# Two layers of segmented attention and gated feed-forward on one core: a new opening, rows of two more norms turned by DMA, a new order of work

## Chip, cores, metric

The kernel runs on one core of a Trainium2 chip. A core has TensorE (PE; its weight loads are listed apart as PEld), VectorE (DVE), ScalarE (ACT), GpSimd (POOL) and SyncE (SP, whose queue issues nearly all transfers here), which run side by side and meet at semaphores. The metric is the device time of one execution in microseconds (us); lower is better.

## What is computed

An input x of 2048 rows and 512 columns (bfloat16) goes through attention, feed-forward, and both again with the same weights, each behind a layer norm without weights and each added to x:

```python
x = x + _A_ref(_layernorm(x, axis=-1), A_wq, A_wk, A_wv, A_wo, A_beta)
x = x + _B_ref(_layernorm(x, axis=-1), B_w_gate, B_w_up, B_w_down)
x = x + _A_ref(_layernorm(x, axis=-1), A_wq, A_wk, A_wv, A_wo, A_beta)
x = x + _B_ref(_layernorm(x, axis=-1), B_w_gate, B_w_up, B_w_down)
```

The attention has 32 heads of 16 columns and takes the rows in 4 segments of 512. Inside a segment it is causal softmax attention; beside it each head reads a 16x16 memory, to which every segment adds phi(k)ᵀ v, where phi(t) is t+1 for positive t and exp(t) otherwise:

```python
for s in range(N):
    logits = jnp.einsum('bhqd,bhkd->bhqk', qs, ks) * scale + mask
    a_dot = jnp.einsum('bhqk,bhkd->bhqd', _softmax(logits, axis=-1), vs)
    a_mem = num / den            # phi(q) @ M,  phi(q) @ z + 1e-6
    outs.append(g * a_mem + (1.0 - g) * a_dot)
    M = M + jnp.einsum('bhld,bhle->bhde', pk, vs)
```

The feed-forward is `_gelu(x @ w_gate) * (x @ w_up) @ w_down` with 1792 hidden columns.

## The kernel before

**Stages.** Layer and segment together give eight stages, k = 0 to 7. `Att(k)` normalizes 512 rows, makes q, k and v, takes 20 score steps, turns exp of the scores into weighted sums of v ("flush"), and reads and updates the memory. `Ffn(k)` multiplies by wo, adds to x, normalizes again and runs gate, up and down. Stage k+4 needs the rows that stage k has finished; the stages of one layer need each other only through the memory.

**How a norm's rows get turned.** A `Norm` has the key ("xnTa", k) for attention and ("xnTf", k) for the feed-forward. Per tile of 128 rows VectorE takes the statistics (L522, L531), GpSimd makes the scales (L539, L545), and VectorE writes the normalized rows xn (L559). Products need them transposed, in xnT. `row()` has two ways for that (L573 to 578). If the key is in `BY_PE`, four products with the identity on TensorE (line 498, in the groups m<-ident,xn) go into the list of items, and VectorE or ScalarE copies the result out of PSUM (L489, L490). Otherwise `turn_later` posts a transposing DMA to SP's queue (L463, xnT<-xn). Stage 0's attention norm is turned by hand in the opening (L602, L605, L607).

**Products.** Nearly all dense products go through `product` (L493 to 498): four matmuls, each a quarter of the array's columns, of up to 512 columns of the other operand. Score matmuls (L941) use another tiling, in which the array is cut by rows. A score step fills two PSUM buffers, st0 and st1, and ScalarE takes exp of each (L972); GpSimd masks the diagonal blocks (L959). The planner may visit both buffers of a step together or one after the other with other products between; the latter is called a halved step here.

**What sets the order.** The program is planned while it is built. `Clocks` keeps a clock for TensorE and one for each other engine (512 columns 0.2158 us, a change of tiling 0.102), and the loop at the end (L1364 to 1400) always asks what is next on TensorE: a score visit if its inputs and buffers are planned to be ready, else a started item, else the first item in order of its due time whose `ready` holds, else half a score step, else a filler, a product of ones (L1395, the group m<-warm of line 498) that keeps TensorE busy. Work for the other engines is posted as jobs with slacks. Due times are `DUE` and `DUE_STEP` by kind plus a correction by stage and index from `BIAS`. What runs on the chip is the resulting fixed order on each engine, with semaphores where one needs another.

**The opening** is written out by hand (L1239 to 1296): loads of x rows 0 to 3, wk and wq in two parts of columns each, x of segment 1, wv, in that order on SP; 19 products of ones (`WARM`, L404); then statistics, scales and rows of stage 0, their turns on TensorE, and the first block of q and k for stage 0. Then the planner's clocks are set by hand (L1292 to 1296) and the loop begins. Statistics of segments 1 and 2 are posted at fixed times (L1306, L1307), and the later loads are posted at fixed times too (L42).

The v item's due time and condition before:

```python
return Item(k - QK_DUE + bias("v", k, j) + DUE["v"] + 0.01 * j if k else -0.61,
            lambda: ck.has(("xnTa", k)) and (k < SETS or ("flush", k - SETS, 3, 1) in ev),
            dense(ps, pairs), done, kind="v", ps=ps)
```

Of the kernel before, what the change touches and what calls it, by code (L numbers as in the profile page):

```python
# [11 lines left out]
ACT = mybir.ActivationFunctionType  # L12
# [6 lines left out]
P = 128  # L19
# [4 lines left out]
NK = 2 * NSEG  # L24
L = 512
# [4 lines left out]
TPS = L // P  # L30
# [2 lines left out]
EPS_LN = 1e-5  # L33
EPS_MEM = 1e-6
MANUAL = {ENG.PE, ENG.Activation, ENG.SP, ENG.DVE, ENG.Pool}
WARM = 19
STEPS = 20
BY_PE = {("xnTf", 0), ("xnTf", 1), ("xnTf", NK - 1)}
M_BANKS = 4
PT_STEPS = 5  # L40
SETS = 3
# [3 lines left out]
N3 = 0.0  # L45
GELU_TILES = 2
QK_DUE = 0.655
E_Q = -0.378
E_K = 1.118

FLUSH_WAIT = 5.905
PIECE_SLACK = 3.609
URGENT, SOON, NORMAL = -11.1, -0.333, 0.0
EXP_SLACK, E_SLACK, PHI_SLACK, GELU_SLACK = -1.031, 6.011, 3.476, 3.142
ACT_EVICT, FIRST_EVICT = 3.886, 2.071
XN_BUFS = 4
XN_KEPT = 0
XNA1_PE = 0
NORM_HALVES = 8
KBP = 0  # L60
XNP = 0
RAWS = [7, 7, 8, 6, 8, 6, 8]
FLUSH_FIRST = -0.616
SECOND_EVICT = 0.639
E_BUFS = 2
KB_SLACK = 4.318
HALF_STEPS = 1
LAST_FIRST = 8
MARGIN = 1.0
PHI_MARGIN = 1.7  # L70
KB_MARGIN = 1.5
MEM_SLACK = -2.669


DUE = {"wo": 0.557, "gate": 1.085, "up": 1.338, "down": 1.877, "upd": 0.195, "mem": 0.129, "v": 0.157}
DUE_STEP = {"gate": 0.0119, "up": 0.0256, "down": 0.0162}
BIAS = {
    **{("qk", *k): d for k, d in {
        (0,): 0.054, (1,): 0.349, (1, 4): -0.115, (2,): 0.05, (3,): 0.031, (4,): -0.046, (5,): -0.12, (6,):
        0.194, (7,): 0.037, (7, 5): -0.014  # L80
    }.items()},
    **{("mem", *k): d for k, d in {
        (0,): -0.022, (0, 0): -0.039, (1,): -0.188, (2,): 0.215, (3,): 0.144, (4,): -0.223, (5,): -0.032,
        (6,): -0.036, (7,): -0.117
    }.items()},
    **{("down", *k): d for k, d in {
        (0,): 0.506, (1,): -0.623, (2,): -0.186, (3,): -0.143, (4,): -0.443, (5,): -0.102, (6,): 0.877, (6,
        2): 0.03, (7,): -0.082
    }.items()},
    **{("upd", *k): d for k, d in {  # L90
        (0,): -0.189, (1,): 1.254, (2,): -0.142, (3,): 1.042, (4,): -0.026, (5,): 0.508, (6,): 0.081, (7,):
        0.007
    }.items()},
    **{("v", *k): d for k, d in {
        (0,): 0.246, (1,): 0.279, (2,): 0.177, (3,): -0.1, (4,): -0.388, (4, 0): -0.03, (5,): -0.816, (6,):
        -0.162, (7,): 0.199
    }.items()},
    **{("wo", *k): d for k, d in {
        (0,): -0.36, (0, 0): -0.225, (1,): 0.135, (2,): -1.075, (3,): -0.773, (4,): -0.197, (5,): -0.803,
        (5, 2): -0.205, (6,): -0.181, (7,): -0.25  # L100
    }.items()},
    **{("gate", *k): d for k, d in {
        (0,): 0.131, (1,): -0.134, (2,): 0.56, (2, 5): 0.034, (3,): 0.122, (4,): -0.775, (4, 8): 0.253,
        (5,): -0.02, (6,): 0.694, (7,): -0.205
    }.items()},
    **{("up", *k): d for k, d in {
        (0,): 0.267, (1,): 0.175, (2,): -0.027, (3,): -0.044, (4,): -0.002, (4, 4): -0.286, (5,): -0.133,
        (6,): -0.52, (7,): -0.092
    }.items()},
    **{("num", *k): d for k, d in {  # L110
        (2, 0): -0.064, (3, 0): -0.003, (3, 2): -0.014, (4, 2): 0.171, (5, 2): -0.092
    }.items()},
    **{("ek", *k): d for k, d in {
        (1, 1): 0.005, (2, 1): -0.028
    }.items()},
    **{("eq", *k): d for k, d in {
        (3, 2): -0.036
    }.items()},
}

# [203 lines left out]
def kernel(  # L324
# [14 lines left out]
    nc = tc.nc  # L339
# [9 lines left out]
    ck = Clocks()  # L349
    ev = ck.ev  # L350
# [52 lines left out]

    keep_warm(WARM, 0)  # L404

# [32 lines left out]
    for va in vaugs:  # L438
        nc.scalar.activation(out=by_head(va)[:, :, :, DH], in_=cden[:].unsqueeze(1).to_broadcast([P, TPS, H]),
                             func=ACT.Copy)  # L440
# [5 lines left out]
    def later_constants():  # L446
# [5 lines left out]

        ck.pool.post(14.0, MEM_SLACK, (1.9, lambda: nc.gpsimd.memset(kBs[2][:], 0.0), None))
        for b in range(4):
            ck.pool.post(20.0 + 3.0 * b, MEM_SLACK, (0.5, lambda b=b: scale(b), None))

# [9 lines left out]
    banks = [0.0] * M_BANKS  # L466
# [13 lines left out]
    def evict(ps, dst, src, told, slack=NORMAL):  # L480
# [6 lines left out]

        first = FIRST_EVICT if ("scores", 0) not in ev else SECOND_EVICT if ("scores", 1) not in ev else ACT_EVICT
        ck.dve.post(ck.made(), slack, (0.673, lambda: nc.vector.tensor_copy(out=dst(), in_=src()), end), taken=taken)  # L489
# [18 lines left out]
    class Norm:  # L508
# [54 lines left out]
        def row(self, j, i, ready):  # L563
# [9 lines left out]
            def told(t):  # L573
                if self.key in BY_PE or XNA1_PE and self.key == ("xnTa", 1):
                    insert(self.turn_item(j, xn, t, landed))
# [43 lines left out]
    class Att:  # L619
# [13 lines left out]
        def add_items(self):  # L633
            k, s = self.k, self.s
# [18 lines left out]
            def q_done(b, ps):  # L653
                def told(t):
                    ev["q", k, b] = t
                    self.q_there[b // 2].append(t)
                    if s > 0 and len(self.q_there[b // 2]) == 2:
                        e_jobs.append((k - E_Q + bias("eq", k, b) + 0.03 * b, max(self.q_there[b // 2]),
                                       lambda: k < 2 or ("memn", k - (1 if s > 1 else 2)) in ev,
# [4 lines left out]
            def odd_heads(t):  # L664
# [11 lines left out]
                for g in range(4):  # L676
                    r = slice(32 * g + 16, 32 * g + 32)
                    ck.sp.post(t, KB_SLACK, (0.55, lambda r=r: nc.sync.dma_start(
                        out=self.kB[r], in_=self.kf[r]), lambda t2: ck.at(t2 + 1.8, lambda: landed(t2 + 2.0))))

            def k_done(b, ps, at=None):
                def told(t):
# [8 lines left out]
                    if s < NSEG - 1:  # L691
                        before = ("mem", k - 1) if s else ("mem", k - 2) if k else ("xnTa", 1)
                        e_jobs.append((k + E_K + bias("ek", k, b) + 0.03 * b, t, lambda: before in ev,
                                       lambda r, sl: self.phi_k(b, r, sl), True))
# [9 lines left out]
            def v(j):  # L704
                ps = Psum()
                pairs = [(lambda kt=kt: self.norm.xnT[:, kt, j * P:(j + 1) * P], lambda kt=kt: w_att["v"][:, kt, :])
                         for kt in range(KT)]

                def done():
                    self.counted()  # L710
                    evict(ps, lambda: by_head(self.vaug)[:, j, :, 0:DH],
                          lambda: ps()[:].rearrange("p (h e) -> p h e", e=DH),
                          lambda t: ev.update({("v", k, j): t}))

                return Item(k - QK_DUE + bias("v", k, j) + DUE["v"] + 0.01 * j if k else -0.61,
                            lambda: ck.has(("xnTa", k)) and (k < SETS or ("flush", k - SETS, 3, 1) in ev),
                            dense(ps, pairs), done, kind="v", ps=ps)

            for b in range(KT) if k else range(EARLY, KT):
# [128 lines left out]
        def upd_item(self):  # L848
# [13 lines left out]
            def done():  # L862
# [23 lines left out]
                else:  # L886
# [5 lines left out]
                             (0.2, z, told)]  # L892
                ck.dve.chain(ck.made(), MEM_SLACK, *steps)

            items.append(Item(k + DUE["upd"] + bias("upd", k), ready, [(Clocks.MM[128], lambda c=c: m(c)) for c in range(n_mm)],
                              done, kind="upd", ps=psm))
# [192 lines left out]
    class Ffn:  # L1089


        def __init__(self, k):
# [6 lines left out]
            self.n_gate, self.n_gel, self.kept = [0] * self.parts, [0] * self.parts, [[] for _ in range(self.parts)]  # L1099
            raw = RAWS[k] if self.parts == 1 else 0  # L1100

# [137 lines left out]
    n0 = att[0].norm  # L1239
# [27 lines left out]
    a0 = att[0]  # L1267
    a0.made()
    n0.first_rows = [n0.normed(j, j) for j in range(2)]
    gate()  # L1270
    n0.first_rows += [n0.normed(2, 2)]
    n0.first_turn(0)
    n0.first_turn(1)
    keep_warm(2, 0)
    ps = bank_tile(1, [P, L])
    a0.first_k(ps, 0, P)
    n0.first_turn(2)
    nc.vector.tensor_copy(out=a0.kf[:, 0, 0:P], in_=ps[:, 0:P])
    n0.first_rows += [n0.normed(3, 3)]
    n0.first_turn(3)  # L1280
    ps, half = bank_tile(2, [P, L]), L // 2
    a0.first_q(ps, 0, half)
    nc.scalar.activation(out=a0.q[:, 0, 0:half], in_=ps[:, 0:half], func=ACT.Copy)
    keep_warm(1, 1)
    ps = bank_tile(0, [P, L])
    a0.first_q(ps, half, L)
    nc.vector.tensor_copy(out=a0.q[:, 0, half:L], in_=ps[:, half:L])
    ps = bank_tile(3, [P, L])
    a0.first_k(ps, P, L)
    nc.scalar.activation(out=a0.kf[:, 0, P:L], in_=ps[:, 0:L - P], func=ACT.Copy)  # L1290
    ev["xnTa", 0] = 0.0
    ck.pe, ck.act.free, ck.dve.free, ck.pool.free, ck.sp.free = 11.7, 12.4, 11.8, 9.0, 9.0  # L1292
    banks[:] = [11.8, 11.1, 11.2, 12.4]
    ev["q", 0, 0] = 11.65
    a0.n_qkv = 2
    a0.k_done(0, None, 12.35)
    streams = [(k, t) for k in range(NK) for t in range(STEPS)]
    later_constants()
    for at, kb, piece in pieces:
        ck.sp.post(at, PIECE_SLACK, (0.57, piece, lambda t, kb=kb: ck.dma_load(t, kb)))  # L1300

    def norm_of_input(s, at, gap):
        for j in range(TPS):
            ck.at(at + gap * j, lambda j=j: att[s].norm.stats(j, ck.pe))

    norm_of_input(1, 12.9, 0.5)  # L1306
    norm_of_input(2, 22.0, 1.0)  # L1307
    if N3:
        norm_of_input(3, N3, 1.0)
# [54 lines left out]
    while streams or items or opened or ck.busy():  # L1364
# [14 lines left out]
        if min(banks) <= ck.pe:  # L1379
            late = ck.pe - (FLUSH_FIRST if ("scores", 0) not in ev else FLUSH_WAIT)  # L1380
            got = next((it for it in items if (it.kind != "flush" or not streams or it.posted < late
# [8 lines left out]
        if min(banks) <= ck.pe:  # L1390

            if streams:
                ps = Psum()
# [37 lines left out]
```

## Time and profile before

| what | value |
|---|---|
| median of 3 runs | 552.38 us (551.13 to 552.74) |
| the profiled execution | 552.22 us, its span from first to last instruction 550.4 |
| TensorE matmuls | 544.2 us busy, 11518 |
| ScalarE | 447.3 us busy, 540 instructions |
| VectorE | 433.4 us busy, 822 instructions |
| GpSimd | 239.2 us busy, 486 instructions |
| DMA | 27.87 MB, mean 51 GB/s; 225 GB/s in the first 14 us |
| transposing DMAs | xnT 48, phik 24, amT 24; 2.5 us from issue to landing in the median |

Busy time is the union of an engine's instructions. In rows of the timeline the columns are start, length, engine, line, operation, output<-inputs and count; in square brackets stands how long the engine was idle before, and what ended that. In groups of lines there is a count, the busy time, the mean of one in ns, and the idle time before. The chain is followed back from the last instruction to what released it.

### The profile page before, as it was taken

Reading aid. Unit: us, or ns where it says so; the run is one execution under the profiler, and the core shown is the slowest. Engines: PE = TensorE matmul, PEld = TensorE weight load, DVE = VectorE, ACT = ScalarE, POOL = GpSimd, SP = SyncE. Lnnn points to the kernel's source line nnn. Section 1 sums busy time; section 2 is a strip of 40 time slices with the busy share of each in tenths; the row PEclk is TensorE's granted clock in tenths of the full one; section 3 lists DMA queues with packets and bytes.
Section 4 is the critical chain, followed back from the end, with each engine's and each line's share of the span. In section 5 each row is a group of like instructions: output and inputs, shape, how many; then the busy total and the mean of one; then the engine's idle time right before and its main releaser. Section 6 shows DMA issues by size and latency. Waiting matters only on the chain.

```text
span 550.4 us, 25623 instructions
## 1 busy us (share of the span) xinstructions
PE 544.2 (99%) x11518; PEld 271.6 (49%) x11518; DVE 433.4 (79%) x822; ACT 447.3 (81%) x540; POOL 239.2 (43%) x486
## 2 busy tenths in 40 slices
PE   7999999999999999999999999999999999999997
PEld 3333445444454444444444444444454445545997
DVE  5878898998779999589877986789778878677162
ACT  4999999998898889987899879897798977974500
POOL 4775562465525565325642464245523572021000
DMA  7357530611104124301230122201521113100001
GB/s 227 36 140 205 111 77 4 169 27 18 34 14 60 22 41 74 56 13 12 42 60 2 32 41 41 42 7 26 89 32 31 22 29 73 23 2 31 14 5 41
DMA packets 65405, 27.87 MB, mean 51 GB/s; under 512 B 54864, under 2 KB 64848, under 8 KB 65296
## 3 DMA queue, kind: packets, MB, share of 16 engines
q1 hardware_dynamic: 65152, 26.23, 22.9%
q8 instruction: 90, 1.47, 1.1%
q14 instruction: 19, 0.16, 0.1%
q10 hardware_dynamic: 144, 0.01, 0.0%
HBM read 9.71 MB, written 2.10 MB: 21 GB/s over the span
## 4 chain that ended last, share of the span: by engine, by line
PE 95%; DMA 1%; DVE 1%; SPq 1%; issue 0%; ACT 0%; DVEq 0%
PE m L498 78%; PE st L941 10%; PE m L1006 7%; DMA wv_sb<-in_A_wv_dram 1%; SPq L361 1%; DVE gel L1193 1%; ACT pt L972 0%; DVE e L766 0%; DVE rdm L798 0%; DVE mblk L871 0%; ACT vaug L490 0%; DVE e L774 0%; DVE x_sb L1104 0%; DVE rdm L795 0%; DVE zcols L874 0%
## 5 line engine op out<-in xcount | busy, mean ns | idle before, releaser
L972 ACT ACTIVATE pt<-st 128x1024 bf16<-128x1024 f32 x320 | 310.1, 1028 | 52.9 <-PE st L941 49.1
L959 POOL TENSOR_SCALAR_AFFINE_SELECT pt<-pt 128x512 bf16<-128x512 bf16 (+2 forms) x416 | 206.8, 513 | 248.1 <-ACT pt L972 231.7
L498 PE MATMUL m<-wd_sb,gel 128*32 128x512 bf16 (+2 forms) x1848 | 107.2, 373 | 0.0
L498 PE MATMUL m<-xnT,wu_sb 128*32 128x512 bf16 (+1 forms) x2016 | 106.9, 356 | 0.2
L498 PE MATMUL m<-xnT,wg_sb 128*32 128x512 bf16 (+1 forms) x2016 | 106.1, 356 | 0.0
L1193 DVE TENSOR_TENSOR gel<-gel,m 128x512 bf16<-128x512 bf16 x112 | 75.0, 681 | 25.5 <-PE m L498 21.7
L498 PEld LDWEIGHTS <-wu_sb 128*32 128x32 bf16 x2016 | 52.1, 97 | 39.1 <-issue 5.5
L498 PEld LDWEIGHTS <-wg_sb 128*32 128x32 bf16 x2016 | 51.6, 97 | 39.6 <-issue 4.8
L498 PEld LDWEIGHTS <-gel 128*32 128x32 bf16 x1848 | 50.5, 97 | 39.6 <-issue 6.3
L1104 DVE TENSOR_TENSOR x_sb<-x_sb,m 128x512 bf16<-128x512 bf16 (+1 forms) x65 | 42.5, 666 | 23.2 <-PE m L498 23.1
L1030 DVE STREAM_TRANSPOSE byq<-m 128x512 f32<-128x512 f32 x64 | 45.2, 707 | 13.4 <-PE m L1006 13.1
L1006 PE MATMUL m<-pt,vaug 128*32 128x256 bf16 (+3 forms) x1088 | 46.4, 293 | 0.0
L1158 ACT ACTIVATE gel<-m 128x512 bf16<-128x512 f32 x62 | 34.3, 603 | 11.1 <-PE m L498 10.9
L522 DVE BATCH_NORM_STATS2 st<-x_sb 128x6 f32<-128x512 bf16 x60 | 40.8, 680 | 0.6
L941 PE MATMUL st<-q,kf 16*128 16x256 bf16 (+3 forms) x544 | 40.0, 294 | 0.0
L941 PE MATMUL st<-q,kB 32*128 32x256 bf16 (+3 forms) x544 | 38.4, 291 | 0.0
L498 PE MATMUL m<-xnT,wk_sb 128*32 128x512 bf16 x496 | 35.6, 381 | 0.0
L1006 PEld LDWEIGHTS <-vaug 128*32 128x32 bf16 x1088 | 25.0, 97 | 21.3 <-issue 5.7
L498 PE MATMUL m<-wv_sb,xnT 128*32 128x512 bf16 x512 | 32.5, 380 | 1.3 <-DMA wv_sb<-in_A_wv_dram 1.2
L941 PEld LDWEIGHTS <-kf 16*128 16x128 bf16 x544 | 12.2, 91 | 43.2 <-issue 42.1
L498 PE MATMUL m<-xnT,wq_sb 128*32 128x512 bf16 x496 | 33.5, 380 | 0.0
L498 PE MATMUL m<-wo_sb,aT 128*32 128x512 bf16 x512 | 31.2, 380 | 0.0
(94 smaller groups left out, 540.8 us busy)
## 6 DMA issues: line engine op xcount, KB each, us to landing
out_dram<-x_sb SPq DMA_DIRECT2D x15, 128.0 KB, 1.7
wg_sb<-in_B_w_gate_dram SPq DMA_DIRECT2D x8, 224.0 KB, 3.6
kB<-kf SPq DMA_DIRECT2D x28, 64.0 KB, 2.6
wu_sb<-in_B_w_up_dram SPq DMA_DIRECT2D x8, 224.0 KB, 4.0
wd_sb<-in_B_w_down_dram SPq DMA_DIRECT2D x7, 256.0 KB, 3.5
x_sb<-in_A_x_dram SPq DMA_DIRECT2D x3, 512.0 KB, 7.0
xnT<-xn SPq DMA_TRANSPOSE x48, 2.5
x_sb<-in_A_x_dram SPq DMA_DIRECT2D x4, 128.0 KB, 3.0
```

The costliest lines, as they stand in the source:

```text
L361: nc.sync.dma_start(out=dst, in_=src)
L498: nc.tensor.matmul(out[r], lhsT=lhsT[:, r], rhs=rhs, start=start, stop=stop, tile_position=(0, 32 * c))
L522: nc.vector.bn_stats(out=self.st6[:, 0, :], in_=x_sb[:, self.tt0 + j, :])
L941: nc.tensor.matmul(sts[j // 2][:, j % 2, c0:c0 + q1 - q0], lhsT=lhsT[rows, b, P * ki:P * ki + P], rhs=self.q[rows, b, q0:q1], start=True, ...
L959: nc.gpsimd.affine_select(out=dv, in_=dv, pattern=[[0, w], [1, P]], compare_op=ALU.is_ge, fill=0.0, base=0, channel_multiplier=-1)
L972: 1.024, lambda st=st, tile2=tile2: nc.scalar.activation(out=tile2[:], in_=st[:], func=ACT.Exp, scale=SCALE), told), table="exp")
L1006: nc.tensor.matmul(ps()[32 * j:32 * j + 32, q0 + shift:q1 + shift], lhsT=self.vaug[:, ki, h * (DH + 1):h * (DH + 1) + 32], rhs=step["pt"][ ...
L1030: nc.vector.transpose(out=self.byq[:, c], in_=ps()[:])
L1104: ck.dve.post(ck.made(), slack, (0.15 + 0.533 * n / D, lambda: nc.vector.tensor_tensor(out=xt, in0=xt, in1=ps()[:, 0:n], op=ALU.add), lamb ...
L1158: return lambda: nc.scalar.activation(out=out(), in_=in_(), func=ACT.Gelu_apprx_tanh)
L1193: ck.dve.post(ck.made(), NORMAL, (0.683, lambda: nc.vector.tensor_tensor(out=hidden(g, h), in0=hidden(g, h), in1=banked(ps), op=ALU.mult), ...
```

## The change

1. `BY_PE` holds ("xnTf", 0) alone. The feed-forward norms of stages 1 and 7 go by transposing DMA.
2. `WARM` is 17, not 19.
3. In the opening row 3 is normalized right after row 2, ahead of the copy of the first part of kf; the turn of row 3 comes behind the first half of q's first block on TensorE; the last part of kf is copied by VectorE, not ScalarE.
4. The v items of stage 0 need a new event "wv", set to 13.4, before the planner may start them. The hand-set clocks are earlier (TensorE 11.4 in place of 11.7), and segment 1's statistics are posted from 12.0 in place of 12.9.
5. All slacks, due times and corrections are new; `BIAS` has many more entries, most of them for single items.

```diff
-WARM = 19
+WARM = 17
-BY_PE = {("xnTf", 0), ("xnTf", 1), ("xnTf", NK - 1)}
+BY_PE = {("xnTf", 0)}
...
-DUE = {"wo": 0.557, "gate": 1.085, "up": 1.338, "down": 1.877, "upd": 0.195, "mem": 0.129, "v": 0.157}
-DUE_STEP = {"gate": 0.0119, "up": 0.0256, "down": 0.0162}
+DUE = {"wo": 0.403, "gate": 1.084, "up": 1.357, "down": 1.717, "upd": 0.191, "mem": 0.165, "v": 0.12}
+DUE_STEP = {"gate": 0.0119, "up": 0.0227, "down": 0.05}
...
-                            lambda: ck.has(("xnTa", k)) and (k < SETS or ("flush", k - SETS, 3, 1) in ev),
+                            lambda: ck.has(("xnTa", k), *([] if k else ["wv"])) and (k < SETS or ("flush", k - SETS, 3, 1) in ev),
...
-    n0.first_rows += [n0.normed(2, 2)]
+    n0.first_rows += [n0.normed(j, j) for j in range(2, TPS)]
     n0.first_turn(0)
     n0.first_turn(1)
     keep_warm(2, 0)
     ps = bank_tile(1, [P, L])
     a0.first_k(ps, 0, P)
+    nc.vector.tensor_copy(out=a0.kf[:, 0, 0:P], in_=ps[:, 0:P])
     n0.first_turn(2)
-    nc.vector.tensor_copy(out=a0.kf[:, 0, 0:P], in_=ps[:, 0:P])
-    n0.first_rows += [n0.normed(3, 3)]
-    n0.first_turn(3)
     ps, half = bank_tile(2, [P, L]), L // 2
     a0.first_q(ps, 0, half)
+    n0.first_turn(3)
     nc.scalar.activation(out=a0.q[:, 0, 0:half], in_=ps[:, 0:half], func=ACT.Copy)
...
     a0.first_k(ps, P, L)
-    nc.scalar.activation(out=a0.kf[:, 0, P:L], in_=ps[:, 0:L - P], func=ACT.Copy)
-    ev["xnTa", 0] = 0.0
-    ck.pe, ck.act.free, ck.dve.free, ck.pool.free, ck.sp.free = 11.7, 12.4, 11.8, 9.0, 9.0
+    nc.vector.tensor_copy(out=a0.kf[:, 0, P:L], in_=ps[:, 0:L - P])
+    ev["xnTa", 0], ev["wv"] = 0.0, 13.4
+    ck.pe, ck.act.free, ck.dve.free, ck.pool.free, ck.sp.free = 11.4, 10.5, 11.9, 9.0, 9.0
...
-    norm_of_input(1, 12.9, 0.5)
+    norm_of_input(1, 12.0, 0.5)
```

More of the change, by code (lines that the diff above doesn't have):

```diff
@@ L47 @@
 QK_DUE = 0.655
[L48 to L55, printed above, removed]
+E_Q = -0.418
+E_K = 1.181
+FLUSH_WAIT = 5.526
+PIECE_SLACK = 3.065
+URGENT, SOON, NORMAL = -12.906, -1.242, 0.0
+EXP_SLACK, E_SLACK, PHI_SLACK, GELU_SLACK = -1.179, 7.675, 2.909, 1.554
+ACT_EVICT, FIRST_EVICT = 5.384, 0.429
 XN_BUFS = 4
@@ L61 @@
 XNP = 0
-RAWS = [7, 7, 8, 6, 8, 6, 8]
-FLUSH_FIRST = -0.616
-SECOND_EVICT = 0.639
+RAWS = [7, 7, 6, 8, 8, 6, 9]
+FLUSH_FIRST = 0.183
+SECOND_EVICT = 0.54
 E_BUFS = 2
-KB_SLACK = 4.318
+KB_SLACK = 9.551
 HALF_STEPS = 1
@@ L71 @@
 KB_MARGIN = 1.5
-MEM_SLACK = -2.669
-DUE = {"wo": 0.557, "gate": 1.085, "up": 1.338, "down": 1.877, "upd": 0.195, "mem": 0.129, "v": 0.157}
-DUE_STEP = {"gate": 0.0119, "up": 0.0256, "down": 0.0162}
+MEM_SLACK = -1.631
+DUE = {"wo": 0.403, "gate": 1.084, "up": 1.357, "down": 1.717, "upd": 0.191, "mem": 0.165, "v": 0.12}
+DUE_STEP = {"gate": 0.0119, "up": 0.0227, "down": 0.05}
 BIAS = {
     **{("qk", *k): d for k, d in {
-        (0,): 0.054, (1,): 0.349, (1, 4): -0.115, (2,): 0.05, (3,): 0.031, (4,): -0.046, (5,): -0.12, (6,):
-        0.194, (7,): 0.037, (7, 5): -0.014
[3 rows of a table added]
@@ L81 @@
     }.items()},
     **{("mem", *k): d for k, d in {
-        (0,): -0.022, (0, 0): -0.039, (1,): -0.188, (2,): 0.215, (3,): 0.144, (4,): -0.223, (5,): -0.032,
-        (6,): -0.036, (7,): -0.117
+        (0,): -0.022, (0, 0): -0.149, (1,): -0.188, (1, 0): 0.051, (2,): 0.396, (3,): 0.144, (3, 0): 0.02,
+        (4,): -0.223, (4, 0): -0.08, (5,): -0.032, (6,): 0.007, (6, 0): 0.022, (7,): -0.133, (7, 0): -0.371
     }.items()},
     **{("down", *k): d for k, d in {
-        (0,): 0.506, (1,): -0.623, (2,): -0.186, (3,): -0.143, (4,): -0.443, (5,): -0.102, (6,): 0.877, (6,
@@ L88 @@
-        2): 0.03, (7,): -0.082
[3 rows of a table added]
     }.items()},
     **{("upd", *k): d for k, d in {
-        (0,): -0.189, (1,): 1.254, (2,): -0.142, (3,): 1.042, (4,): -0.026, (5,): 0.508, (6,): 0.081, (7,):
-        0.007
+        (0,): -0.189, (0, 0): 0.123, (1,): 1.267, (1, 0): 0.412, (2,): -0.142, (3,): 1.042, (3, 0): -0.028,
+        (4,): -0.026, (4, 0): 0.114, (5,): 0.556, (5, 0): 0.037, (6,): 0.239, (7,): 0.058, (7, 0): 0.002
     }.items()},
     **{("v", *k): d for k, d in {
-        (0,): 0.246, (1,): 0.279, (2,): 0.177, (3,): -0.1, (4,): -0.388, (4, 0): -0.03, (5,): -0.816, (6,):
@@ L96 @@
-        -0.162, (7,): 0.199
[3 rows of a table added]
     }.items()},
     **{("wo", *k): d for k, d in {
-        (0,): -0.36, (0, 0): -0.225, (1,): 0.135, (2,): -1.075, (3,): -0.773, (4,): -0.197, (5,): -0.803,
-        (5, 2): -0.205, (6,): -0.181, (7,): -0.25
+        (0,): -0.262, (0, 0): -0.225, (1,): 0.387, (1, 1): 0.021, (2,): -1.075, (3,): -0.773, (4,): -0.298,
+        (5,): -0.803, (5, 2): -0.205, (6,): -0.051, (7,): -0.25
     }.items()},
     **{("gate", *k): d for k, d in {
-        (0,): 0.131, (1,): -0.134, (2,): 0.56, (2, 5): 0.034, (3,): 0.122, (4,): -0.775, (4, 8): 0.253,
@@ L104 @@
-        (5,): -0.02, (6,): 0.694, (7,): -0.205
[4 rows of a table added]
     }.items()},
     **{("up", *k): d for k, d in {
-        (0,): 0.267, (1,): 0.175, (2,): -0.027, (3,): -0.044, (4,): -0.002, (4, 4): -0.286, (5,): -0.133,
-        (6,): -0.52, (7,): -0.092
+        (0,): 0.267, (1,): 0.175, (2,): -0.027, (2, 9): 0.111, (3,): -0.044, (3, 4): 0.038, (3, 6): -0.041,
+        (4,): -0.002, (4, 4): -0.453, (4, 5): -0.033, (5,): -0.112, (6,): -0.52, (7,): -0.092, (7, 2):
+        -0.133, (7, 9): 0.102
     }.items()},
@@ L110 @@
     **{("num", *k): d for k, d in {
-        (2, 0): -0.064, (3, 0): -0.003, (3, 2): -0.014, (4, 2): 0.171, (5, 2): -0.092
[4 rows of a table added]
     }.items()},
     **{("ek", *k): d for k, d in {
-        (1, 1): 0.005, (2, 1): -0.028
[4 rows of a table added]
     }.items()},
     **{("eq", *k): d for k, d in {
-        (3, 2): -0.036
[3 rows of a table added]
     }.items()},
@@ L1289 @@
     a0.first_k(ps, P, L)
-    nc.scalar.activation(out=a0.kf[:, 0, P:L], in_=ps[:, 0:L - P], func=ACT.Copy)
-    ev["xnTa", 0] = 0.0
-    ck.pe, ck.act.free, ck.dve.free, ck.pool.free, ck.sp.free = 11.7, 12.4, 11.8, 9.0, 9.0
-    banks[:] = [11.8, 11.1, 11.2, 12.4]
-    ev["q", 0, 0] = 11.65
+    nc.vector.tensor_copy(out=a0.kf[:, 0, P:L], in_=ps[:, 0:L - P])
+    ev["xnTa", 0], ev["wv"] = 0.0, 13.4
+    ck.pe, ck.act.free, ck.dve.free, ck.pool.free, ck.sp.free = 11.4, 10.5, 11.9, 9.0, 9.0
+    banks[:] = [11.3, 10.3, 10.3, 12.0]
+    ev["q", 0, 0] = 11.3
     a0.n_qkv = 2
-    a0.k_done(0, None, 12.35)
+    a0.k_done(0, None, 11.95)
     streams = [(k, t) for k in range(NK) for t in range(STEPS)]
```

24 rows, old and new, of the table BIAS are left out of this document.

## The prediction

> **What bounds the kernel now.** I read the page's busy line and chain first, then the table of windows, then the list of waits, and then the timeline at four places: the opening, and the places where rows of a norm are turned on TensorE.
>
> ```profile
> PE 544.2 (99%) x11518; PEld 271.6 (49%) x11518; DVE 433.4 (79%) x822; ACT 447.3 (81%) x540; POOL 239.2 (43%) x486
> ...
> PE 95%; DMA 1%; DVE 1%; SPq 1%; issue 0%; ACT 0%; DVEq 0%
> ```
>
> The chain that ends last is TensorE for 95% of the span. A share of busy time is an average, so the windows come next (the columns are the window, its length, and the busy time and instruction count of each engine):
>
> ```profile
> 0.00:14.00 14.00, 11.21 (x62) 5.14 (x62) 7.46 (x22) 6.04 (x11) 5.86 (x19) 1.00 0.76 225
> 14.00:77.00 63.00, 63.00 (x1116) 25.47 (x1113) 52.66 (x107) 61.40 (x76) 41.55 (x89) 1.00 0.51 117
> ...
> 497.00:550.40 53.40, 50.23 (x1488) 43.03 (x1480) 23.05 (x40) 13.15 (x20) 3.09 (x5) 1.00 0.08 23
> ```
>
> From 14 to 77 us TensorE has no gap at all, and ScalarE is busy for 61.4 of 63 us. After 14 us all six windows asked for are full on TensorE to within 3.4 us, of which 3.1 is the addition and the store behind the last product (547.3 to 550.4). So the time is a sum: what TensorE executes, at its own pitch, plus the opening. A change counts only if it takes something out of that queue, adds to it, or makes its head wait.
>
> Busy is not the same as useful. Three things in the queue are not work of the reference. **Filler**: the planner puts a product of ones where it has nothing ready, and the group m<-warm of line 498 has 48 matmuls, that is 12 products. Two long down stretches in the chain differ by one product of four matmuls, and 2.49 less 2.27 is 0.22 us; 12 of them are 2.6 us. **Halved score steps**: score matmuls need another tiling of the array than the rest. In the opening a product begins at 13.36, a score visit at 13.69, the next product at 14.02; each of the two took 0.33 us for 0.22 of work, so a change of tiling is 0.11 and a visit 0.22. The timeline has 177 separate stretches of line 941 and the code 160 steps, so 17 steps were taken in two visits: 17 x 0.22 = 3.7 us. **Turned rows**: 192 matmuls m<-ident,xn for three norms.
>
> The opening is the one place where TensorE stands:
>
> ```profile
> 4.79 0.96 SPq L361
> 5.80 7.52 DMA wv_sb<-in_A_wv_dram
> 14.09 2.27 PE m L498 x40
> ```
> ```profile
> 11.38 0.81 PE L901 MATMUL m<-xnT,wk_sb 128*128 128x384 bf16 x4
> 13.36 0.40 PE L498 MATMUL m<-wv_sb,xnT 128*32 128x512 bf16 x4 [1.17 <-DMA wv_sb<-in_A_wv_dram]
> ```
>
> The chain begins with a load: wv lands at 13.32, the first products written behind the opening are v products, and TensorE stands from 12.19 to 13.36 for them.
>
> **Part by part. The wait for wv.** The v items of segment 0 now need ("wv"), set to 13.4, so the planner must put something else first: the q and k products of blocks 1 to 3, six items of four products, 6 x 0.87 us. Their weights were issued at 3.69 and 4.25 and take 5.6 and 6.1 us to land (9.3 and 10.4), long before. The 1.17 us of standing are filled. What is late next is the first score, which needs kf.
>
> **The opening's order.** Two warm products fewer: at the end of the row they start 0.22 apart, so the queue is free 0.43 earlier, but row 0 is normalized only at about 7.45 and its turn ran at 7.85; that is worth 0.2 to 0.4 at most. The larger part is row 3. In the trace its normalization stood behind the copy of kf, its turn on TensorE waited 0.5 us for it (10.01), and the first half of q stood behind that turn:
>
> ```profile
> 9.34 0.29 DVE L1278 CAST kf<-m 128x128 bf16<-128x128 f32 x1 [0.48 <-PE m L901]
> 9.55 0.41 DVE L559 TENSOR_SCALAR xn<-x_sb,mv,rs 128x512 bf16<-128x512 bf16 x1
> ...
> 10.01 0.40 PE L602 MATMUL m<-ident,xn 128*128 128x128 bf16 x4 [0.48 <-DVE xn L559]
> ```
>
> Now row 3 is normalized right behind row 2 (8.85 to 9.27), q's first half runs at about 9.4 to 9.8, row 3 is turned at 9.8, copied by VectorE until 10.6, and q's second half starts at about 10.65, where the trace has 10.93. Line 901 then ends at 11.9, not 12.19. The last copy of kf goes from ScalarE (0.49) to VectorE; between 0.42 for 256 columns and 0.69 for 512 that is 0.55, so kf is there at about 12.5, not 12.71, and the first exp can start 1.2 us earlier than 14.12. The queue proper starts at 11.9 in place of 13.36: **-1.5 us**. Bounds: -1.2 (only the standing goes) to -1.9 (both warm products count too). The other operands are the same.
>
> On the clock: warm products start 0.427 us apart up to 6.20 and 0.216 from 6.55 on, so the last six of the 19 run fast and the change cuts two of those. [...]
>
> **Rows by DMA.** Norms 1 and 7 lose TensorE's turns, 0 keeps them. In the timeline eight such products (32 matmuls, two rows) begin at 501.31 and what follows them begins at 501.76: 0.45 us. A norm has four rows, so two norms give 4 x 0.45 = **-1.8 us**. Turns and dense products share a tiling (128*32), so no switch goes with them. Eight evictions of 0.59 to 0.69 us go too, from engines that are not the bound: nothing. Added are eight transposes on SP, 1.2 to 1.3 us each to issue, 2.5 us (at most 4.8) to land. The gate products wait for the landing. Covers, from the old order:
>
> ```profile
> 134.57 0.90 DVE L559 TENSOR_SCALAR xn<-x_sb,mv,rs 128x512 bf16<-128x512 bf16 x2 [0.28 <-POOL rs L545]
> ...
> 141.23 1.04 PE L498 MATMUL m<-xnT,wg_sb 128*32 128x512 bf16 x16
> ```
> ```profile
> 510.36 0.73 DVE L559 TENSOR_SCALAR xn<-x_sb,mv,rs 128x512 bf16<-128x512 bf16 x2
> ...
> 515.54 0.55 PEld L498 LDWEIGHTS <-xn 128*32 128x32 bf16 x32
> ```
>
> Norm 1: the rows are ready between 133.3 and 135.5; four issues of 1.3 from 133.7 end the last landing at about 140.1, or 142.4 with the slowest landing. The first gate product was at 141.2. SP issues no transpose between 121.7 and 145.5 there, so nothing is ahead of them; scores and q, k products of later segments cover a lateness of 1 us. Norm 7, first half: rows ready at 498.9 to 499.5, landed by 503, needed at 509.5. Second half: ready at 510.7 and 511.1, landed by 514.7 (517 at worst), and TensorE turned them only at 515.5; were they later, 14 groups of the first half's up products stand ready there, about 12 us by the trace for both halves, so 6 for one. Queued behind these transposes on SP are stores of x_sb that nobody waits for before the end. Without all cover each late microsecond costs one.
>
> **The order planned anew.** The trace cannot show it. What it can give back is bounded by the non-work: 2.6 filler and 3.7 halved steps, together -6.3. Upwards each more costs 0.22; the nearest rows are the same counts, so a doubling of the filler gives +2.6. I take -0.7: of the filler half may go (-1.3), since six of the twelve, between 73 and 77 us, stand among the turns of norm 0 and could give way to another order; and 0.6 comes back, because segment 1's statistics start 0.9 earlier by the diff (12.9 to 12.0) while TensorE starts 1.5 earlier, and the other six fillers (25 to 29 us) stand where its rows land (25.8 to 28.5).
>
> **Sum.** Profiled execution 552.2 (span 550.4 and 1.8 around it): 552.2 - 1.5 - 1.8 - 0.7 = **548.2**. The median shown is 552.38, 0.2 above; I leave the forecast on the profiled one.
>
> **Rivals.** (a) *The turns' time doesn't come back.* Gate products find rows that have not landed, the planner fills with ones, and 1.8 us of turns become 1.8 of filler; the re-plan gives nothing. For it: the landing of row 4 of norm 1 at 140.1 to 142.4 against a need at 141.2. Against it: q, k and down products around it. Time 552.2 - 1.5 = 550.7. 0.12.
>
> (a') *A full TensorE row is no bound*, and work taken from it gives nothing: the same 550.7, by the same subtraction. Against it: matmuls start at a steady pitch, and the list of waits has 1.2 us for a matmul's longest wait, the wv one. 0.02. [...]
>
> (b) *The re-plan takes much of the bound*: two thirds of the 6.3 go, 552.2 - 3.3 - 4.2 = 544.7. For it: every such product is planned, none forced by the chip. Against it: from 14 to 77 us ScalarE has 97%, so TensorE lacks work there whatever the order. 0.14.
>
> (c) *Slower.* More score steps are halved. The planner takes a half when a score buffer is free and nothing else ready, most of them in the stage from 25 to 80 us, where ScalarE frees one buffer per microsecond; TensorE arriving 1.5 us sooner finds buffers taken more often. Each costs 0.22. To end at 553.9 the forecast must lose 5.7, 26 more halved steps (43 in place of 17); two segments have 40 steps. Time 554. Against it: ScalarE's exps start 1.2 us sooner too. 0.05.
>
> (d) *Nothing moves*: the opening shifts and the fillers at 25 to 29 take it all back (+1.5), the rest as forecast: 549.7, inside the range. 0.12.
>
> **Numbers.** 0.3% of 552.4 is 1.7 us, what a measurement of this kernel can tell from no change: faster is below 550.7. Forecast 0.55 and (d) 0.12, nearly all faster; (a) and (a') 0.14, at the boundary, mostly within; (b) 0.14; (c) 0.05. Faster 0.80, same 0.14, slower 0.06. The range goes from near (b) to (a): 545.0 to 551.0, with half of (b), a third of (a) and (c) outside.
>
> **What would show it.** Right: the first L498 matmul of wq or wk, not wv, at about 11.9; no entry of TensorE waiting for wv; m<-ident,xn down from 192 to 64 matmuls, xnT<-xn from 48 to 56 transposes; the m<-warm group of L498 at 30 to 50 matmuls, line 941 in 165 to 180 stretches. Wrong: TensorE waits on xnT near 135 to 145 or 515 to 525 us, or the warm group and the score stretches grow by more than the 3.3 us saved.

## The result, and the profile after

The changed kernel takes 553.77 us in the median of 20 runs, the kernel before 551.82 in 20 runs beside them. The ratio is 1.0028, with a 95% interval of 1.0018 to 1.0037: a little slower, where 4 us less was forecast. Its executions spread over 4.5 us (551.69 to 556.16), those of before over 1.6. The profiled one took 553.48 us, with a span of 551.4.

The busy line and the chain of the changed kernel's page:

```profile
PE 543.4 (99%) x11376; PEld 271.1 (49%) x11376; DVE 424.4 (77%) x809; ACT 448.8 (81%) x546; POOL 237.4 (43%) x486
...
PE 85%; DVE 9%; DMA 3%; issue 1%; ACT 1%; POOL 1%
```

TensorE has 142 instructions fewer (128 matmuls of turns, 12 of filler, 2 warm ones) and is as full as before, but other engines and DMA now hold 15% of the chain, not 5%. The opening, from the timeline:

```profile
10.93 0.81 PE L915 MATMUL m<-xnT,wk_sb 128*128 128x384 bf16 x4
11.68 0.40 PE L955 MATMUL st<-q,kf 16*128 16x512 bf16 x4
12.00 1.05 PE L512 MATMUL m<-xnT,wq_sb 128*32 128x512 bf16 x16
```

No wait for wv is left, and the planner's order starts at 11.68 in place of 13.36. The windows show where the gain went. In a row stand the window, its length, the busy time and count of PE, PEld, DVE, ACT and POOL, then the granted clock, the busy share of DMA and its GB/s. The kernel before had 63.00 in the first of these windows, and in the three others:

```profile
77.00:128.00 51.00, 51.00 (x1092) 24.14 (x1091) 47.21 (x86) 48.84 (x60) 23.92 (x46) 1.00 0.27 63
128.00:165.00 37.00, 37.00 (x864) 18.11 (x857) 29.02 (x57) 33.33 (x43) 15.76 (x36) 1.00 0.14 24
165.00:440.00 275.00, 274.77 (x5660) 128.03 (x5659) 230.10 (x427) 238.57 (x282) 130.45 (x269) 1.00 0.22 37
```

The changed kernel has:

```profile
14.00:77.00 63.00, 62.95 (x1124) 25.63 (x1120) 55.06 (x109) 61.40 (x78) 43.27 (x90) 1.00 0.49 115
77.00:128.00 51.00, 50.35 (x1060) 23.54 (x1056) 42.54 (x81) 48.14 (x59) 22.72 (x44) 1.00 0.29 65
128.00:165.00 37.00, 36.78 (x828) 17.56 (x823) 29.87 (x60) 34.52 (x45) 17.34 (x36) 1.00 0.37 56
165.00:440.00 275.00, 273.96 (x5592) 127.97 (x5588) 220.94 (x411) 239.09 (x286) 126.18 (x266) 1.00 0.22 35
```

And from the list of waits (who waited for whom; us in total, how often, the longest):

```profile
PE m L512 <- DMA xnT<-xn: 0.6, 2, 0.4
PE st L955 <- ACT pt L986: 0.5, 1, 0.5
```

TensorE now stands between 77 and 440 us: for rows that DMA turned, for score buffers, and in two waits of 0.3 us for results of VectorE. To count it whole, I took every product of the trace from its start to the start of the next and set it against its usual pitch; what is more than 0.06 us over that is a wait. This sorting is my own reckoning from the starts in the trace; no view prints it. It finds more than the list, which counts only the time in which no matmul runs. A few matmuls are missing from each trace and look like waits here, so the difference of the waits is good to about 0.3 us. From the first instruction of the planner's order to TensorE's last end:

| TensorE, us | before | changed | difference |
|---|---|---|---|
| opening, until the planner's order starts | 13.36 | 11.68 | -1.68 |
| products of the reference | 447.33 | 447.33 | 0 |
| turns of rows | 2.69 | 0.90 | -1.79 |
| filler | 2.59 | 1.94 | -0.65 |
| score matmuls | 37.76 | 39.04 | +1.28 |
| changes of tiling | 36.92 | 37.94 | +1.02 |
| waits | 1.81 | 4.33 | +2.52 |
| small rest | 4.85 | 4.62 | -0.23 |
| behind the last product | 3.10 | 3.67 | +0.57 |
| span | 550.4 | 551.4 | +1.0 |

Score work is the same, so +1.28 there and +1.02 in tilings are the price of halved steps: the timeline has 182 stretches of score matmuls, before 177, which is 22 halved steps in place of 17. That is 0.46 us for each net additional stretch, a quotient of totals and twice what I had taken. The timeline of the kernel before shows why:

```profile
25.51 0.39 PE L941 MATMUL st<-q,kf 16*128 16x512 bf16 x2
25.83 0.61 PE L498 MATMUL m<-warm 128*32 128x512 bf16 x8
```

A half visit of two matmuls takes 0.32 us until the next product starts, as long as the visit of four at 13.69 (0.33): the four run side by side (they start 3 to 4 ns apart, at 13.69 to 13.70, and last 384 ns each, 0.39 us together), so half of them saved nothing here.

### The profile page after: what moved, and what is told of

Its sections match the earlier page's. It is cut to its first block, busy times and chain, and to the rows that moved or that the text cites. A ratio compares the mean times of both kernels' runs of the same rounds, so it can differ in the third digit from the quotient of the medians.

```text
span 551.4 us, 25353 instructions
## 1 busy us (share of the span) xinstructions
PE 543.4 (99%) x11376; PEld 271.1 (49%) x11376; DVE 424.4 (77%) x809; ACT 448.8 (81%) x546; POOL 237.4 (43%) x486
## 4 chain that ended last, share of the span: by engine, by line
PE 85%; DVE 9%; DMA 3%; issue 1%; ACT 1%; POOL 1%
PE m L512 69%; PE st L955 9%; PE m L1020 6%; DMA xnT<-xn 2%; DVE x_sb L1118 2%; DVE st L536 1%; DVE byq L1044 1%; ACT pt L986 1%; DVE ab L1052 1%; DMA x_sb<-in_A_x_dram 1%; POOL rs L559 1%; DVE phiq L761 1%; DVE xn L573 0%; DVE st L1260 0%; DVE aT L1063 0%
## 5 line engine op out<-in xcount | busy, mean ns | idle before, releaser
L512 PE MATMUL m<-xnT,wq_sb 128*32 128x512 bf16 x496 | 34.8, 381 | 0.0
L512 PE MATMUL m<-xnT,wk_sb 128*32 128x512 bf16 x496 | 33.3, 380 | 0.3 <-DVE byq L1044 0.3
```

The source lines that it names most:

```text
L512: nc.tensor.matmul(out[r], lhsT=lhsT[:, r], rhs=rhs, start=start, stop=stop, tile_position=(0, 32 * c))
```

## The experiments

Theory A: the opening and the rows pay what was forecast, but the order that was planned around them has more halved steps and waits, and eats the gain. Theory B: the rows by DMA land late and TensorE waits for them. Theory C came up with the first traces: standing costs more than its own time. All ratios are to the kernel before, run on the same chip; brackets hold the 95% interval. Counts of "planned" halved steps are the planner's and include halves with nothing between them.

**Stage 7's rows alone.**

```diff
-BY_PE = {("xnTf", 0), ("xnTf", 1), ("xnTf", NK - 1)}
+BY_PE = {("xnTf", 0), ("xnTf", 1)}
```

> The kernel before with one edit: stage 7's feed-forward rows by DMA instead of TensorE. Theory A (the parts pay, the order planned around them eats it): here the planner makes the same order but for the missing turns (as many halved score steps, 22 planned, and 12 fillers), so the full 0.9 us of one norm's turns comes off: 0.9 us less than before, about 550.9. Theory B (rows by DMA land late and TensorE waits for them): no gain or a loss, 551.8 or more, with TensorE waiting on xnT between 510 and 525 us.

Measured: 551.06 us, ratio 0.9986 [0.9978, 0.9995], 0.85 less than before (551.91). The order of score steps is the same (177 stretches). So the turns taken out do come back: the interval means 0.3 to 1.2 us, and theory A had 0.9. Theory B is not void, though. In the profiled execution (551.53) the gates of the second half waited, as the timeline says:

```profile
517.29 2.91 PE L498 MATMUL m<-xnT,wg_sb 128*32 128x256 bf16 x100 [0.89 <-DMA xnT<-xn]
```

The last transpose was issued at 513.29 us and landed at 517.15, 3.9 us later, not 2.5.

**Both rows, old settings.** `BY_PE` as in the change, nothing else.

> The kernel before with the rows of stages 1 and 7 both by DMA, old settings, old opening. 1.8 us of turns go. Theory A: the planner's own order gets 2.1 us longer on its clock (25 halved steps planned in place of 22, 4.4 us of planned standing in place of 1.4), so the chip is about 2 us slower than before, near 553.9. Theory B: also slower, but by waits of TensorE on DMA xnT near 140 us, not by halved steps or planned waits for banks. If rows by DMA alone decide and the order does not matter: 550.0.

Measured: 554.49 us, ratio 1.0053 [1.0037, 1.0069]. As theory A has it: 2.6 us slower although 1.8 us of turns went, and the waits of its profile near 206 us are for score buffers, none for xnT near 140. The eight executions at a granted clock of 0.999 or 1.0 have a median of 554.2, near the 553.9 of theory A. The profiled one is the longest (557.53), one of three at 0.994, and its windows show something else (the column behind the counts is the granted clock):

```profile
204.00:208.00 4.00, 2.90 (x66) 1.29 (x58) 3.96 (x8) 4.00 (x6) 2.76 (x5) 0.99 0.70 75
208.00:214.80 6.80, 6.80 (x64) 1.90 (x66) 2.93 (x6) 3.84 (x5) 2.40 (x6) 0.50 0.49 96
```

TensorE stood for 1.1 of 4 us, and then ran at half its clock for 6.8 us.

**The opening alone.** The opening's hunks, `WARM` and the v condition; old settings, old `BY_PE`.

> The kernel before with only the new opening (17 warm products, row 3 earlier, v behind wv, clocks, statistics of segment 1 at 12.0), old settings, turns of stages 1 and 7 on TensorE. The queue proper starts 1.7 us earlier as in the changed kernel's trace. Theory A: the order behind it gets 3.0 us longer on the planner's clock (24 halved steps, 4.4 us of standing), so about 1.3 us slower than before, 553.1. Theory B (the loss is with the DMA rows, of which none are added here): 1.7 us faster, 550.1.

Measured: 555.48 us, ratio 1.0060 [1.0044, 1.0075]. No DMA row was added, so theory B cannot make this. Its order starts at 11.32. One execution of the six ran at a granted clock of 1.0 and took 553.2, what theory A gave; the five others ran at 0.997 and took 555.4 to 556.7. The profile, one of those five, in windows:

```profile
101.00:104.30 3.30, 2.14 (x28) 0.77 (x32) 3.30 (x7) 3.30 (x4) 1.84 (x4) 1.00 0.89 191
104.30:107.70 3.40, 3.40 (x40) 1.24 (x36) 2.16 (x5) 2.60 (x4) 1.75 (x5) 0.50 1.09 257
```

Two waits for score buffers, 0.65 and 0.52 us, and then 3.4 us at half clock: 1.7 us more that no plan holds. Its score matmuls come in 177 stretches, as before, so what is lost here beside the clock does not show as more stretches. The expectation had 4.4 us of planned standing, and the list of waits has 1.4 us for score buffers, in three waits, where before has none.

**The changed kernel again**, on two later occasions, both on one chip.

> The changed kernel once more, on the same chip as the three others, for a second profile: its times spread over 4.5 us, those of before over 1.6. About 553.8. Theory A: 28 planned halved steps and the same planned standing in every execution, so the loss after the opening is the same 2.1 us at least, and what varies is small. Theory B: the waits of gate products on DMA xnT (0.4 at 143 us and 0.4 at 398 us in the first profile) move from execution to execution and make up most of the loss.

Measured: 552.10 us (551.59 to 556.76), ratio 1.0016 [0.9999, 1.0033]. Its profiled execution took 552.04: the same 182 stretches, turns and filler, but 2.70 us of waits where the first profile had 4.33, with none for xnT. So a fixed part of the loss (halved steps, planned waits) and a part that moves with the landings: A and B both.

> The changed kernel itself on the same chip as the two new orders, so that they can be set against it and not only against before. 552.1 to 553.8, by its two earlier medians; spread of 4 us or more.

Measured: 552.50 us (551.22 to 556.50), ratio 1.0017 [1.0001, 1.0034]. The profiled execution was the longest, 556.50, and shows what the tail of the spread is made of. (In the three sets of the changed kernel all five executions above 555 us have a granted clock of 0.994 to 0.997, all others 0.998 to 1.0.) Timeline and windows:

```profile
398.12 1.43 PE L512 MATMUL m<-xnT,wg_sb 128*32 128x512 bf16 x16 [1.71 <-DMA xnT<-xn]
```
```profile
396.30:398.60 2.30, 0.59 (x17) 0.32 (x16) 1.31 (x2) 1.65 (x2) 1.34 (x4) 1.00 0.42 59
398.60:405.50 6.90, 6.90 (x88) 2.47 (x80) 2.89 (x5) 2.56 (x3) 1.00 (x3) 0.51 0.34 76
```

Stage 5's fourth row landed 4.9 us after its issue at 393.10; the gate product behind it waited 1.71 us (0.41 in the first profile, none in the second), and the clock halved for 6.8 us. Stage 5 went by DMA before the change too; there its rows landed at 393.8 and nothing waited. The new order asks for them earlier than they surely come.

**Without fillers.** To test theory C alone: products of ones that compute nothing are left out of the kernel before.

```diff
-                product(ps()[:], warm[:], wide)
                 ck.on_pe(Clocks.MM[512])
```

> The kernel before with one edit: the 12 filler products behind the opening are left out (they compute nothing of the reference), the order of everything else is the same. In the trace of before six of them stand between 25.2 and 28.8 us (1.3 us of TensorE's time in 3.6) and six between 73.4 and 77.1. Theory C (a cluster of standing of about 1 us within 3.4 halves TensorE's clock for one or two stretches of 3.4 us, as the clock records of the second and third experiment show at 208 and 104 us): the clock falls near 28 or 77 us in part of the executions, each time costing up to 1.7 us or 3.4, so the median is 1 to 4 us above before, 553 to 556, at a granted clock of 0.994 to 0.997. Rival (standing costs only its own time, and a filler saves nothing): 551.8 within 0.5, granted clock 0.999 to 1.0 as before.

Measured: 557.29 us, ratio 1.0093 [1.0070, 1.0117]. But the expectation was wrong in one point: with the product the planner also lost its change of tiling, and its order behind 25 us was another one. So once more, with the order kept:

```diff
-                product(ps()[:], warm[:], wide)
+                ck.tiling("columns")
                 ck.on_pe(Clocks.MM[512])
```

> The earlier kernel without fillers had lost the planner's change of tiling with them, so its order behind 25 us was another one. Here only the 12 filler products (48 matmuls) are gone and the order of every other instruction is that of the kernel before. Theory C: as much standing as the fillers took (1.3 us between 25 and 29, 1.3 between 73 and 77), and the clock halves for 3.4 or 6.8 us behind the first cluster, the second or both: 1.7 to 5 us above before, 553.5 to 557, granted clock 0.991 to 0.997. If the other order alone made that kernel slow: 551.9 within 0.7, granted clock 0.999 to 1.0.

Measured: 554.17 us (553.01 to 557.57), ratio 1.0032 [1.0014, 1.0050], granted clock 0.991 to 0.996 in all nine executions, where before had 0.997 to 1.0. Timeline and windows of its profile, the longest of them:

```profile
25.60 0.39 PE L941 MATMUL st<-q,kf 16*128 16x512 bf16 x2 [0.49 <-ACT pt L972]
26.52 0.39 PE L941 MATMUL st<-q,kf 16*128 16x384 bf16 x4 [0.53 <-ACT pt L972]
...
28.17 1.04 PE L498 MATMUL m<-xnT,wq_sb 128*32 128x512 bf16 x8 [0.28 <-DMA xnT<-xn]
```
```profile
20.00:27.00 7.00, 5.99 (x96) 2.23 (x92) 6.90 (x17) 7.00 (x9) 4.91 (x13) 1.00 0.42 63
27.00:34.00 7.00, 6.72 (x72) 1.77 (x64) 5.21 (x11) 5.35 (x7) 5.61 (x11) 0.58 0.47 124
...
77.00:84.00 7.00, 6.06 (x92) 2.32 (x92) 5.85 (x11) 5.79 (x8) 3.71 (x7) 0.76 0.28 59
```

Leaving out 2.6 us of useless products made the kernel 1.6 us slower. Where the fillers had been, TensorE stood, and in the profiled execution half clock followed at both places; the clock of the other eight says the same. The granted clocks of 0.58 over 27 to 34 us, 0.93 over 34 to 41 and 0.76 over 77 to 84 make 10.2 us at half clock; these are 5.1 us lost, and 557.57 less 5.1 is 552.5, the time of before. In this kernel the filler is not waste.

**The same parts, other orders.** The opening and the rows by DMA are those of the change; slacks, due times and corrections are others, searched for a shorter order on the planner's clock.

```diff
-DUE = {"wo": 0.403, "gate": 1.084, "up": 1.357, "down": 1.717, "upd": 0.191, "mem": 0.165, "v": 0.12}
+DUE = {...}
...
-RAWS = [7, 7, 6, 8, 8, 6, 9]
+RAWS = [7, 7, 6, 7, 10, 5, 6]
...
```

> The changed kernel with its opening and its rows by DMA untouched; only the slacks, due times and corrections are others, found by trying many for a shorter planned order: 22 halved steps planned in place of 28, 178 visits for 182, 2.75 us shorter on the planner's clock; its planned standing near 90 to 105 us is that of the changed kernel. Theory A (the parts pay, the order ate it): 2.7 us below the changed kernel, about 550.3 on a chip where before has 551.9, granted clock 0.999 to 1.0 in most executions. Rival (the two parts themselves do not pay on the chip): no faster than before, 552 or more, whatever the order.

Measured: 549.63 us (549.0 to 550.96), ratio 0.9964 [0.9953, 0.9975]: 2.3 us below before, 2.9 below the changed kernel on the same chip. Its profile has 178 stretches of score matmuls, and in its list of waits no matmul waits for a row that DMA turned; only weight loads do, for 0.6 us in two waits. Theory A's 550.3 was a little too careful.

> As the other new order (same opening, same rows by DMA), but planned with 1.6 us instead of 1.0 between a transpose's planned landing and its use, and with less planned standing (1.85 in place of 2.45; 14 fillers in place of 9). On the planner's clock 2.1 us shorter than the changed kernel and 0.7 longer than the other new order. Theory A alone: 550.9. Theory B (waits on landings and standing that halves the clock are the chip's own addition): shorter than the tight order in spite of its planner, 549.5 to 550.5, and a smaller spread of the executions than 4 us.

Measured: 550.32 us (549.74 to 550.98), ratio 0.9969 [0.9959, 0.9980]. Its planner asks for 0.7 us more than the tight order's, and that is what it takes; the spread is 1.2 us against 2.0. So the margin buys no time; that it buys steadiness is suggested by twelve executions of each, not shown. Theory B as a reason by itself falls: the tight order keeps the margin of the changed kernel and is fast.

## Why the prediction was wrong, point by point

The range of 545.0 to 551.0 was missed. Of the signs named in advance, those of the parts came true: no wait for wv, 64 turns, 56 transposes, 36 matmuls of filler. Of the order, 182 stretches lie outside the 165 to 180, and a wait on xnT of 0.22 us came at 143.3.

**The opening, -1.5: right** (-1.68). The order on TensorE went as worked out, a little sooner. A detail was wrong: what starts first is a score visit at 11.68, since step 0 needs only the first 128 columns of kf, which are copied early, not all of kf.

**The rows, -1.8: right as a term** (-1.79 in the table; 0.85 for one norm's 0.9 in the first experiment). The cover was misjudged: norm 1's last row landed at 143.2, where 142.4 was the slowest case I gave, and stage 7's last row at 516.5 in the changed kernel and 517.2 in the first experiment, where 517 was.

**The order planned anew, -0.7: this is the step that failed.** The profiled execution has +3.94 there: -0.65 of filler, +2.30 for five more stretches of score matmuls, +2.52 of waits, and -0.23 of small rest. The second profile (span 549.9) leaves +2.3 by the same subtraction. I had taken the order as nearly free, with a bound upwards of 2.6 that I made by doubling the filler, and left waits out of the bound. The experiments show that it is the order: the old settings with both norms' rows alone or the opening alone gave 2.6 and 3.6 us more than before, 1.7 of the latter by the clock, and other settings with both parts gave 2.3 less. Stage 7's rows alone, which left the order of score steps as it was, gained. Even the best order found keeps 2.3 of the 3.3 us of the parts, so the -0.7 was not reached by any run. The rival "more steps are halved" had half of the mechanism, with 0.22 us for each in place of 0.46, 26 more of them in place of five, and no waits beside them. The 0.22 was the two changes of tiling alone; the score matmuls of the second visit were left out. The count of 17 was too low as well: the planner had 22 halves before and 28 after, and halves that stand next to each other make one stretch.

**"Each late microsecond costs one": wrong.** Standing of 1.17 us cost 1.7 more by the clock in the opening alone (3.4 us at half); 1.1 us with both rows (6.8 at half) and 1.71 us in the third set (6.8) cost 3.4 more each. The 0.89 us of the first experiment, at a granted clock of 1.0, cost only itself. The one profiled execution of the changed kernel above 555 us is of that kind, and the clock of the four others points the same way. The median of the first set is not explained by it: its 17 executions at 0.999 or 1.0 have a median of 553.48.

**Behind the last product** came 0.6 us that nothing foresaw. The last store but one landed 2.46 us after its issue, where before has 1.83; in the two later profiles it took 2.49 and 2.82, with 3.79 and 3.87 us from the last product to the end. The last store's issue on SP took 1.16 us, where before has 0.59, but 0.33 in the third profile, whose tail is as long. Why is open.

That the changed kernel lies 2 us above before in its first 20 runs and 0.2 to 0.6 on two later occasions is not settled either. Its waits differ by 1.6 us between two profiles, in part for xnT (0.6 us of standing in the first, none in the second). Whether the chip makes the difference is not shown: the two later occasions were on one chip, and that of the first set is not on record.

## What to carry to other kernels

Where one engine is full and runs a planned order, an edit is two edits: the part, and the order that is rebuilt around it; price the second by waits and repeated set-up (here 0.46 us for a step in two visits), and expect a part that disturbs the order to lose until the order is fitted again; a part that leaves it alone can gain at once. A sum of removed instructions is what a new order may come near. Try to keep TensorE occupied where it must wait, with products of ones if need be: here leaving out 2.6 us of them cost 1.6 us with the order kept, and in four of the profiles standing of 0.9 to 1.7 us was followed by half clock for 3.4 or 6.8. The order with more time for slow landings took 0.7 us more here; what it may buy is fewer long executions.

## What the runs showed of the hardware

Half clock followed standing of 0.65 and 0.52 us within 1.6 us (the opening alone: a granted clock of 0.50 from 104.3 to 107.7 us), of 1.1 within 4 (both rows: 0.50 from 208.0 to 214.8), of 0.49, 0.53 and 0.28 within 3.1 (without fillers, order kept: 0.58 over 27 to 34 and 0.93 over 34 to 41), and of 1.71 at once (the third set: 0.51 over 398.6 to 405.5). It did not follow the 1.17 us at the opening of the kernel before (the ten products from 14.02 on took 2.34 us together, 0.22 from one start to the next), nor 0.89 at once in the first experiment (1.0 over the span), nor 0.14 and 0.50 that lie 4 us apart in the first profile of the changed one (1.00 over 77 to 128). So in these runs this is a risk, not a threshold. Nearly the same standing could go either way: without fillers and with the order kept TensorE stood for 0.94 us between 77 and 84 us and had a clock of 0.76 there, while the first kernel without fillers stood for 0.93 between 33 and 80, at 0.99, and had 1.00 from 80 to 86.

The stretches at half clock lasted 3.4 us in the opening alone, 6.8 with both rows and 6.8 in the third set (0.51 over 6.9). Why there are two lengths, and what decides whether standing is followed by one, is not shown.

A transposing DMA of 128 rows by 512 columns landed 2.4 us after its issue at the quickest, before and after the change. Of those of xnT 18 of 48 took 3.0 us or more before, at most 4.8, and 25 of 56 in the changed kernel, at most 4.4, at any place in a row of four (3.96, 2.45, 4.37 and 3.80 for its stage 1). The one that TensorE waited 1.71 us for in the third set took 4.9.
